# First projection, input vector and first value sums of a decode attention block on one Trainium2 core

wq is loaded in five transfers of 12-KB rows instead of two, x as one row that the TensorE turns, and the first head's value sums are issued one chunk earlier.

## Chip, cores, metric

The kernel runs on 1 core of one Trainium2 chip. The metric is the time of one execution in microseconds of device time (us), given as the median of several executions. Profiles are of one execution each.

## The reference, cut

```python
# x [1,1,640]; k_cache, v_cache [1,32,32768,192]; wq [640,6144]; wo [6144,640]; w1 [640,1536]; w2 [1536,640]; all bf16
q = (layernorm(x) @ wq).reshape(1, 1, 32, 192).transpose(0, 2, 1, 3)
p = softmax(einsum("bhqd,bhkd->bhqk", q, k_cache) * 192 ** -0.5)
h = x + einsum("bhqk,bhkd->bhqd", p, v_cache).transpose(0, 2, 1, 3).reshape(1, 1, 6144) @ wo
out = h + relu(layernorm(h) @ w1) @ w2
```

One token attends to 32,768 cached keys in each of 32 heads. Keys and values are 805 MB of the 825 MB that are read, and each of these bytes is used once.

## The kernel before

All large loads are issued by one queue (SP). A head's keys come in two loads of 6 MB (`kt[0]`, `kt[1]`), its values in four loads of 3 MB that share two buffers (`vt[0]`, `vt[1]`). A head is worked off in eight chunks: some of the keys of a chunk are turned and scored on TensorE (PE), the others are scored on VectorE (DVE); ScalarE (ACT) takes the exponentials, and PE adds up the values. `PV h, c` is the event "value sum of head h, chunk c is done" and frees a value buffer.

wq is first put into buffers that the head loop uses later: four fifths in `kt[1]`, the last fifth in `vt[1]`. So head 0's second key load waits until the query matmuls have read wq (event `att0`).

```python
wq_c = [kt[1][:, c * H * Dh:(c + 1) * H * Dh] for c in range(DT - 1)] + [vt[1][:, 0:H * Dh]]   # DT = 5

def dma_program(g):
    ...
    def keys(h, ld):
        if h > 0:
            g.wait("PV", h - 1, 4 * ld + 1)
            g.wait("scs", h - 1, 4 * ld + 3)        # VectorE's scores of these keys
        elif ld == 1:
            g.wait("att0")
        load(kt[ld][:], rows(k_hd, h, P * JK * ld, JK), f"dk{ld}", "k", h, ld)

    def vals(h, ld):
        ...
        elif ld > 1:
            g.wait("PV", h, 2 * ld - 3)             # value load 2 waits for sum 1
    ...
    n = (DT - 1) * H * Dh
    load(kt[1][:], wq_view[:, 0:n], "dwq0", "wq", 0)                       # 48-KB rows
    load(vt[1][:, 0:H * Dh], wq_view[:, n:n + H * Dh], "dwq1", "wq", 1)    # 12-KB rows
    for h in range(LAST):
        keys(h, 0); ...; vals(h, 0); keys(h, 1); vals(h, 1); vals(h, 2)    # cut to the order of head 0
        ...

def act_start(g):
    g.do(lambda: act.dma_start(out=x_row[:], in_=A_x.rearrange("b s (c p) -> (b s c) p", p=P)), "dx", ("x",), by=16)
    g.do(lambda: act.dma_start(out=x_pc[:], in_=A_x.rearrange("b s (p c) -> (b s p) c", p=P)), "dx2", ("x_pc",), by=16)
    ...

def queries(g):
    for c in range(DT):
        if c == 0 or c == DT - 1:
            g.wait("wq", min(c, 1))
        calls = [mmul(o_ps[0:HE, 2 * h + e:2 * h + e + 1], wq_c[c][:, h * Dh + e:(h + 1) * Dh:2],
                      ln_t["ln1"]["xn"][:, c:c + 1], ...) for h in range(H) for e in range(2)]   # 64 of 96 columns
        ...

SUMS = ((), (-2,), (-1,), (0, 1), (), (2,), (3,), (4, 5))   # which value sums follow the transposes of chunk c
def pe_head(g, h, turn=None):
    for c in range(NC):
        transposes(g, h, c)
        ...
        for d in SUMS[c]:
            if d >= 0:
                values(g, h, d)
            elif h > 0:
                values(g, h - 1, NC + d)
        scores_pe(g, h, c)
        ...
```

The softmax here doesn't subtract the row's maximum and nothing guards it: scores larger than these inputs give would overflow.

## Time and profile before

| | before |
|---|---|
| median of the first three runs | 1930.16 us (1930.06 to 1931.16) |
| span of the profiled run | 1927.6 us |
| PE, VectorE, ACT busy | 81%, 81%, 50% |
| share of the main DMA queue | 99.4% |
| rate from 100 to 1880 us | 433 GB/s |
| rate from 40 to 52 and from 68 to 80 us | 228 and 280 GB/s |

The prediction shows the lines behind this table. The table of stretches for each window gives every engine's busy time, the granted clock of TensorE (the part of full speed that it was allowed), the DMA share and the rate.

### The profile page before, as it was taken

How to read it: one execution, taken by the hardware profiler on the slowest of the kernel's cores; microseconds unless marked ns; L12 is line 12 of the kernel's file. 1: busy time of each engine (PE TensorE's matmuls, PEld its weight loads, DVE VectorE, ACT ScalarE, POOL GpSimd, SP SyncE). 2: the span in 40 equal slices, each digit the busy share in tenths (PEclk: the TensorE clock that was granted, in tenths of full speed). 3: DMA queues.
4: the chain of work that ended last, by engine and by line, in shares of the span. 5: the costliest groups of instructions: out<-in, count | busy, mean ns of one | idle time of the engine just before them, and what ended most of it. 6: DMA issues, size and time to landing. Idle time of an engine off the chain costs nothing.

```text
span 1927.6 us, 36148 instructions
## 1 busy us (share of the span) xinstructions
PE 1562.3 (81%) x15900; PEld 1102.7 (57%) x15900; DVE 1560.0 (81%) x732; ACT 956.8 (50%) x2000; POOL 1.0 (0%) x6
## 2 busy tenths in 40 slices
PE   5887887888878878779788778788798797787887
PEld 5655555655655555556556556555565565555565
DVE  0988887987878878789788879888788787897895
ACT  0654544544554545545455445545455454554463
POOL 0000000000000000000000000000000000000000
PEclk9888888778788788888788888888887887987898
DMA  8999999999999999999999999999999999999998
GB/s 360 392 433 428 438 432 427 440 429 431 439 428 434 438 428 438 433 428 437 433 429 437 430 432 437 430 435 435 429 438 432 429 438 429 432 438 428 433 433 356
DMA packets 33818, 825.29 MB, mean 428 GB/s; under 512 B 3716, under 2 KB 5252, under 8 KB 8708
## 3 DMA queue, kind: packets, MB, share of 16 engines
q1 hardware_dynamic: 33642, 824.98, 99.4%
q8 instruction: 15, 0.25, 0.0%
q14 instruction: 7, 0.06, 0.0%
q10 hardware_dynamic: 154, 0.00, 0.0%
HBM read 824.97 MB, written 0.00 MB: 428 GB/s over the span
## 4 chain that ended last, share of the span: by engine, by line
DMA 55%; PE 32%; DVE 7%; ACT 5%; SPq 1%; issue 1%; POOLq 0%; DVEq 0%; ACTq 0%
DMA kt<-in_A_k_cache_dram 53%; PE o_ps L369 18%; PE tp L388 9%; ACT kT L610 5%; PE sp L369 3%; DVE pr L691 3%; DVE sc L694 3%; SPq L230 1%; DMA x_pc<-in_A_x_dram 1%; DMA w_s<-in_B_w_dram 1%; PE attT L369 1%; PE mm L369 0%; POOLq L351 0%; DVEq L65 0%; ACTq L642 0%
## 5 line engine op out<-in xcount | busy, mean ns | idle before, releaser
L691 DVE TENSOR_TENSOR pr<-kt,qb 128x2304 f32<-128x2304 bf16 (+2 forms) x257 | 755.9, 2941 | 292.8 <-POOLq L326 243.5
L610 ACT COPY kT<-tp 128x1024 bf16<-128x1024 bf16 (+1 forms) x899 | 817.6, 989 | 299.0 <-PE tp L388 297.2
L388 PE MATMUL tp<-ident_f,kt 128*128 128x128 f32 x3459 | 584.2, 337 | 234.2 <-POOLq L351 232.7
L694 DVE TENSOR_REDUCE sc<-pr 128x12 f32<-128x2304 f32 (+2 forms) x257 | 755.3, 2939 | 8.9
L388 PEld LDWEIGHTS tp<-ident_f,kt 128*128 128x128 f32 x3459 | 508.4, 175 | 241.1 <-POOLq L351 238.0
L369 PE MATMUL o_ps<-vt,pB 128*2 128x384 bf16 x2286 | 460.7, 352 | 5.2 <-POOLq L351 4.4
L369 PE MATMUL o_ps<-vt,pA 128*2 128x384 bf16 x1778 | 330.6, 326 | 0.0
L616 ACT ACTIVATE pB<-sp 128x20 bf16<-128x20 f32 (+2 forms) x258 | 47.8, 185 | 568.0 <-PE sp L369 568.0
L369 PEld LDWEIGHTS o_ps<-vt,pB 128*2 128x2 bf16 x2286 | 187.6, 88 | 230.2 <-issue 92.0
L369 PEld LDWEIGHTS sp<-qm,kT 128*128 128x128 bf16 x6918 | 192.4, 98 | 178.2 <-ACT kT L610 134.7
L369 PE MATMUL sp<-qm,kT 128*128 128x2 bf16 x6918 | 214.3, 164 | 98.2 <-ACT kT L610 96.9
L369 PEld LDWEIGHTS o_ps<-vt,pA 128*2 128x2 bf16 x1778 | 150.1, 84 | 142.8 <-issue 5.1
L625 ACT ACTIVATE pA<-sc 128x12 bf16<-128x12 f32 (+2 forms) x257 | 53.4, 208 | 39.1 <-DVEq L65 38.3
L616 ACT ACTIVATION_READ_ACCUMULATOR pB<-sp 128x1 f32 x258 | 50.2, 195 | 0.0
L625 ACT ACTIVATION_READ_ACCUMULATOR pA<-sc 128x1 f32 x257 | 48.9, 190 | 0.0
L705 DVE TENSOR_SCALAR o_pair<-o_ps,rec 2x384 bf16<-2x384 f32 x32 | 19.4, 605 | 6.3 <-PE o_ps L369 1.7
L369 PE MATMUL o_ps<-xn_ln,kt 128*96 128x1 bf16 (+1 forms) x316 | 22.4, 208 | 0.0
L369 PEld LDWEIGHTS o_ps<-xn_ln,kt 128*96 128x96 bf16 (+1 forms) x316 | 22.2, 176 | 0.1
L369 PE MATMUL mm<-st_ln,mean_mat 128*128 128x2 f32 (+1 forms) x4 | 0.9, 304 | 19.7 <-DVE sq_ln L722 19.4
L369 PE MATMUL attT<-oT,wo_s 128*128 128x1 bf16 x465 | 16.3, 164 | 0.3 <-DVE oT L715 0.3
L369 PEld LDWEIGHTS mm<-dsums,ones_mat 128*128 128x128 f32 x64 | 15.9, 305 | 0.3 <-issue 0.3
L715 DVE TENSOR_SCALAR oT<-mm,odd 128x3 bf16<-128x3 f32 x32 | 7.1, 223 | 10.5 <-PE mm L369 8.1
(69 smaller groups left out, 156.0 us busy)
## 6 DMA issues: line engine op xcount, KB each, us to landing
vt<-in_A_v_cache_dram SPq DMA_DIRECT2D x126, 3072.0 KB, 19.0
kt<-in_A_k_cache_dram SPq DMA_DIRECT2D x62, 6144.0 KB, 32.6
kt<-in_A_k_cache_dram SPq DMA_DIRECT2D x3, 3072.0 KB, 20.3
wo_s<-in_A_wo_dram SPq DMA_DIRECT2D x16, 480.0 KB, 9.5
kt<-in_A_wq_dram SPq DMA_DIRECT2D x1, 6144.0 KB, 17.5
vt<-in_A_v_cache_dram SPq DMA_DIRECT2D x2, 1536.0 KB, 13.5
kt<-in_A_k_cache_dram SPq DMA_DIRECT2D x1, 1920.0 KB, 27.9
kt<-in_A_v_cache_dram SPq DMA_DIRECT2D x2, 960.0 KB, 18.3
```

Of the source, the lines that this page charges most:

```text
L230: g.do(lambda: nc.sync.dma_start(out=dst, in_=src), sem, label, by=16)
L369: return lambda: pe.matmul(o, lhsT=w, rhs=r, **kw)
L388: calls.append(lambda b=b, o=o: pe.transpose(out=dst[:, b, :], in_=src[:, o:o + 2 * P].bitcast(f32), identity=ident_f[:]))
L610: g.do(lambda: act.copy(out=kT[c % 2][:, b0:b0 + nb, :], in_=src[:, 0:nb, :].bitcast(bf16)), "act_pe", ("cp", h, c, k))
L616: g.do(lambda: act.activation(out=pB[c % NB][:, 0:jp], in_=sp[:, 0:jp], func=F.Exp, scale=SCALE, accum_out=dsums[:, 2 * c + 1:2 * c + 2]), ...
L625: g.do(lambda: act.activation(out=pA[c % NB][:, 0:jd], in_=sc[c % NC][:, 0:jd], func=F.Exp, scale=SCALE, accum_out=dsums[:, 2 * c:2 * c + ...
L691: g.chain(lambda: dve.tensor_tensor(out=pr[:, 0:j1 - j0, :], in0=src[:, (off + j0) * Dh:(off + j1) * Dh].rearrange("p (j d) -> p j d", d=D ...
L694: g.chain(lambda: dve.reduce_sum(out=sc[c % NC][:, j0:j1], in_=pr[:, 0:j1 - j0, :], axis=X), "dve")
L705: g.do(lambda: dve.tensor_scalar_mul(out=o_pair[:, :, 1, :], in0=o_ps[0:2, 0:2 * Dh].rearrange("q (i d) -> q i d", i=2), scalar1=rec[0:2, ...
L715: g.do(lambda: dve.tensor_scalar_mul(out=oT[:], in0=mm[:, 0:3], scalar1=odd[:]), "dve_pe", ("oTc", h))
```

## The change

The intent is to start the queries sooner. x then no longer has to arrive in 128 pieces of 10 bytes, the query matmuls begin on the first fifth of wq, and head 0 frees its value buffer one chunk sooner.

```diff
-    x_row = sbuf("x_row", [DT, P], bf16)
-    x_pc = sbuf("x_pc", [P, DT], bf16)
+    x_row = sbuf("x_row", [1, D], bf16)
+    xx = sbuf("xx", [P, 2 * DT], f32)
+    x_pc, x_col = xx[:, 0:DT], xx[:, DT:2 * DT]
 ...
-                g.wait("PV", h - 1, 4 * ld + 1)
+                g.wait("PV", h - 1, 2 if h == 1 and ld == 0 else 4 * ld + 1)
 ...
-        n = (DT - 1) * H * Dh
-        load(kt[1][:], wq_view[:, 0:n], "dwq0", "wq", 0)
-        load(vt[1][:, 0:H * Dh], wq_view[:, n:n + H * Dh], "dwq1", "wq", 1)
+        for c in range(DT):
+            load(wq_c[c], wq_view[:, c * H * Dh:(c + 1) * H * Dh], f"dwq{c}", "wq", c)
 ...
-            if c == 0 or c == DT - 1:
-                g.wait("wq", min(c, 1))
+            g.wait("wq", c)
 ...
-            for d in SUMS[c]:
+            for d in (SUMS[c] if h > 0 or c > 5 else ((), (0,), (1,), (), (2,), ())[c]):
 ...
     def pe_start(g):
         g.wait("identf")
+        g.wait("x")
+        cols = [x_row[0:1, c:D:DT] for c in range(DT)] + [x_row[0:1, c * P:(c + 1) * P] for c in range(DT)]
+        pe_group(g, [mmul(mm[:, i:i + 1], col, ident_b[0:1, 0:1], start=True, stop=True) for i, col in enumerate(cols)],
+                 ("xT",), "pe_dve")
         pe_norm(g)
         g.wait("xn", "ln1")
-        g.wait("x")
-        pe_group(g, [lambda: pe.transpose(out=mm[:, 0:4].bitcast(bf16)[:, 0:DT], in_=x_row[:], ...)], ("xT",), "pe_dve")
 ...
-        g.do(lambda: act.dma_start(out=x_row[:], in_=A_x.rearrange("b s (c p) -> (b s c) p", p=P)), "dx", ("x",), by=16)
-        g.do(lambda: act.dma_start(out=x_pc[:], in_=A_x.rearrange("b s (p c) -> (b s p) c", p=P)), "dx2", ("x_pc",), by=16)
+        g.do(lambda: act.dma_start(out=x_row[:], in_=A_x.rearrange("b s d -> (b s) d")), "dx", ("x",), by=16)
 ... (VectorE: one copy of the ten columns to xx; the norm reads its first five)
```

The longer wait of head 1's first key load is a consequence of the third part. With the old order, sum 1 followed the transposes of chunks 0 to 3, which read `kt[0]`. Now only sum 2 does.

More of the change, by code (lines that the diff above doesn't have):

```diff
@@ L182 @@
     odd = sbuf("odd", [P, 1], f32)
-    x_col = sbuf("x_col", [P, DT], f32)
     h_col = sbuf("h_col", [P, DT], f32)
@@ L219 @@
     names = ["pool_pe", "act_pe", "dve_pe", "act_dve", "dve_act", "dve", "dve_row", "pe_dve", "pool_row", "pool_dve", "pool_act", "pe_act", "pe", "dve_sp"]
-    names += [f"dk{i}" for i in range(NK)] + [f"dv{i}" for i in range(NV)] + ["dwq0", "dwq1", "dwo", "dx", "dx2", "dout"]
+    names += [f"dk{i}" for i in range(NK)] + [f"dv{i}" for i in range(NV)] + ["dwo", "dx", "dout"] + [f"dwq{i}" for i in range(5)]
     names += [f"dke{i}" for i in range(4)] + ["dvh"] + [f"dve{i}" for i in range(4)] + ["dw1"] + [f"dw2_{i}" for i in range(3)]
@@ L530, in pe_start @@
         g.wait("identf")
+        g.wait("x")
+        cols = [x_row[0:1, c:D:DT] for c in range(DT)] + [x_row[0:1, c * P:(c + 1) * P] for c in range(DT)]
+        pe_group(g, [mmul(mm[:, i:i + 1], col, ident_b[0:1, 0:1], start=True, stop=True) for i, col in enumerate(cols)],
+                 ("xT",), "pe_dve")
         pe_norm(g)
         g.wait("xn", "ln1")
-        g.wait("x")
-        pe_group(g, [lambda: pe.transpose(out=mm[:, 0:4].bitcast(bf16)[:, 0:DT], in_=x_row[:],
-                                          identity=ident_b[0:DT, 0:DT])], ("xT",), "pe_dve")
         queries(g)
@@ L539, in pe_start @@
         g.wait("qe")
-        g.wait("x_col")
         q_spread(g, 0)
@@ L720, in dve_norm @@
         t = ln_t[tag]
-        g.chain(lambda: dve.reduce_sum(out=t["st"][:, 0:1], in_=col[:], axis=X), "dve_row")
-        g.chain(lambda: dve.scalar_tensor_tensor(out=t["sq"][:], in0=col[:], scalar=1.0, in1=col[:], op0=A.mult,
+        g.chain(lambda: dve.reduce_sum(out=t["st"][:, 0:1], in_=col, axis=X), "dve_row")
+        g.chain(lambda: dve.scalar_tensor_tensor(out=t["sq"][:], in0=col, scalar=1.0, in1=col, op0=A.mult,
                                               op1=A.mult, accum_out=t["st"][:, 1:2]), "dve_row", ("st", tag))
@@ L731, in dve_norm @@
         g.wait("rs", tag)
-        g.do(lambda: dve.tensor_scalar(out=t["xn"][:], in0=col[:], scalar1=t["mv"][:, 0:1], scalar2=t["rs"][:],
+        g.do(lambda: dve.tensor_scalar(out=t["xn"][:], in0=col, scalar1=t["mv"][:, 0:1], scalar2=t["rs"][:],
                                        op0=A.subtract, op1=A.mult), "dve_pe", ("xn", tag))
@@ L740, in dve_start @@
         g.do(lambda: dve.tensor_copy(out=ident_f[:], in_=ident_b), "dve_pe", ("identf",))
-        g.wait("x_pc")
+        g.wait("xT")
+        g.chain(lambda: dve.tensor_copy(out=xx[:], in_=mm[:, 0:2 * DT]), "dve_row")
         dve_norm(g, "ln1", x_pc)
-        g.wait("xT")
-        g.chain(lambda: dve.tensor_copy(out=x_col[:], in_=mm[:, 0:4].bitcast(bf16)[:, 0:DT]), "dve_row", ("x_col",))
     def dve_head(g, h):
@@ L765, in dve_end @@
         t = ln_t["ln2"]
-        g.chain(lambda: dve.scalar_tensor_tensor(out=h_col[:], in0=attT[:, 0:DT], scalar=1.0, in1=x_col[:], op0=A.mult,
+        g.chain(lambda: dve.scalar_tensor_tensor(out=h_col[:], in0=attT[:, 0:DT], scalar=1.0, in1=x_col, op0=A.mult,
                                                  op1=A.add, accum_out=t["st"][:, 0:1]), "dve_row", ("h_col",))
```

## The prediction

> **What bounds the kernel now.** I read the page first, then the table of stretches (busy time by engine, granted clock, DMA share and rate in windows that I chose), then the timeline of the queue that issues transfers, and last the chain of waits and the landing times for the start.
>
> ```profile
> PE 1562.3 (81%) x15900; PEld 1102.7 (57%) x15900; DVE 1560.0 (81%) x732; ACT 956.8 (50%) x2000; POOL 1.0 (0%) x6
> ...
> q1 hardware_dynamic: 33642, 824.98, 99.4%
> ```
>
> No compute engine is over 81% busy, while one DMA queue, which carries all the keys and values, fills 99.4% of the sixteen DMA engines' span. The time is set by how long 825 MB take, plus the stretches in which nothing is moved. The table of stretches finds those:
>
> ```profile
> 2.00:40.00 38.00, 19.16 (x234) 19.09 (x235) 1.93 (x13) 1.51 (x2) 0.00 (x0) 1.00 1.01 425
> 40.00:52.00 12.00, 11.04 (x115) 10.71 (x114) 3.30 (x2) 3.40 (x7) 0.00 (x0) 1.00 0.60 228
> 52.00:68.00 16.00, 10.29 (x123) 9.34 (x123) 15.49 (x6) 11.28 (x24) 0.00 (x0) 0.68 0.98 421
> 68.00:80.00 12.00, 9.56 (x106) 6.53 (x106) 11.54 (x5) 5.87 (x14) 0.00 (x0) 0.93 0.72 280
> 80.00:100.00 20.00, 19.77 (x187) 12.31 (x185) 16.96 (x6) 10.37 (x21) 0.00 (x0) 0.87 1.01 431
> 100.00:1880.00 1780.00, 1455.48 (x14709) 1019.98 (x14709) 1482.97 (x671) 906.21 (x1893) 0.00 (x0) 0.84 1.00 433
> ```
>
> The last column is GB/s, the one before it the DMA share. From 100 to 1880 us the rate is flat at 433 with a share of 1.00. Only two stretches fall short: 40 to 52 us (228 GB/s) and 68 to 80 us (280 GB/s). Against 433 they lose 12 x 205/433 = 5.68 us and 12 x 153/433 = 4.24 us; the recovery after the first (52 to 68, 421 GB/s) loses 16 x 12/433 = 0.44 us more. That is **10.4 us of holes in all**, and the most that a change at the start can win. The ramp of the first 38 us (38 x 8/433 = 0.7 us) is there either way.
>
> The issue timeline says what each hole waits for:
>
> ```profile
> 1.90 0.42 SPq L230 DMA_DIRECT2D kt<-in_A_k_cache_dram  x1
> 2.37 0.77 SPq L230 DMA_DIRECT2D vt<-in_A_v_cache_dram  x1
> 47.34 0.33 SPq L230 DMA_DIRECT2D kt<-in_A_k_cache_dram  x1
> 47.71 26.13 SPq L230 DMA_DIRECT2D vt<-in_A_v_cache_dram  x2
> 73.88 0.43 SPq L230 DMA_DIRECT2D wo_s<-in_A_wo_dram  x1
> 74.36 0.43 SPq L230 DMA_DIRECT2D kt<-in_A_k_cache_dram  x1
> ```
>
> The second key load of head 0 is issued only at 47.34, because its buffer holds wq until the query matmuls have read it; everything issued earlier has landed by 2.37 + 42.7 = 45.1 us (issue plus the landing time that the list of issues gives). The next wait lasts to 73.9 us: the third value load needs the buffer that value sum 1 of head 0 releases, and the stream issued at 47 us ran out at 47.71 + 25.7 = 73.4 us. The chain of waits shows why the queries are late:
>
> ```profile
> 1.54 17.35 DMA x_pc<-in_A_x_dram
> ...
> 21.40 0.18 PE mm L534
> 21.58 25.70 PE o_ps L369 x320
> ```
>
> 1.2 KB of x take 17.35 us to land; the normalisation takes the 2.5 us to 21.4, and 320 query matmuls take 25.70 us. The wq load, landing beside x, would not let them start earlier either:
>
> ```profile
> kt<-in_A_wq_dram SPq DMA_DIRECT2D x1, 6144.0 KB, 17.5
> vt<-in_A_wq_dram SPq DMA_DIRECT2D x1, 1536.0 KB, 20.6
> ```
>
> Issued at 0.96, its 6 MB are there at 18.5 us, as one semaphore.
>
> **What the Trainium skill says.** "DMA: Bandwidth & Descriptors", section "Queues, rings and completion order": each engine goes round-robin between the queues that have work, switching only at packet boundaries. This fits the 17.35 us for 1.2 KB: 128 elements of 10 bytes over 16 engines are 8 turns, and if each waits for one 48-KB row of wq (49,152 B at 433/16 = 27 GB/s: 1.82 us) that is 14.5 us plus start and landing. The same page, "Where 436 GB/s comes from", puts the ceiling of the fabric at 435 GB/s; the trace's 433 is at it, so nothing but the holes can be won. Its section "Why small descriptors are slow (HBM only)" names a fixed cost per packet; no trace of before shows 12-KB rows at length except the fifth of wq, so I estimate them as 1 to 2% slower than 48-KB rows. "TensorE: Matmul & The Clock Gate", section "LDWEIGHTS (loading the stationary operand)": the load goes by columns, not rows. The trace has a weight load of 5 x 128 at 0.10 us and its matmul at 0.18 us, so a one-row load should cost the same 0.10 us.
>
> **The change part by part.**
>
> *x.* One row, one issue, taken in few packets rather than 128. The ACT queue issues it at 0.91, ahead of wq by a hair; I expect it to land by 2 to 3.5 us (estimate: at most one or two 12-KB rows of 0.46 us ahead of it). Ten pairs of 0.10 us load and a matmul are 1.0 to 1.3 us after the identity at 2.78; one copy is 0.2 us; then the same chain from the first sum to xn, 21.35 - 18.91 = 2.44 us. xn is ready near 6.5 to 7 us instead of 21.35.
>
> *wq.* Each fifth is 1.57 MB or 3.63 us at 433 GB/s. Since four fifths landed at 18.5, the first lands near 18.5 - 3 x 3.63 = 7.6 us, the others at 11.2, 14.9, 18.5, 22.2. Each fifth's 64 matmuls take 25.70/5 = 5.14 us, slower than the loads, so after the first no wait remains: the queries run from 7.6 to 33.3 us (before: 47.28), at the granted clock of 1.00 that the table shows for the whole of 2 to 52 us. The buffer is released at 33.5 and the second key load is issued there, 11.6 us before the stream of 45.1 us runs dry. **Hole 1 (5.68 + 0.44 us) closes.** The 12-KB rows cost 1 to 2% of 14.5 us: +0.2 us.
>
> *Stream of head 0 after this.* Key load 0 lands as before, 1.90 + 35.7 = 37.6, with the 0.2 of wq 37.8; values 0 at 45.3, keys 1 (6.29 MB, 14.5 us) at 59.8, values 1 (7.3 us) at 67.1. Compute of head 0, which began at 48.67, begins at 38.0 on the landing of the keys.
>
> *Value sums one chunk earlier.* In before, sum 1 ended at 73.47, which is 24.8 us after VectorE's first product at 48.67. With the old order it would now end at 38.0 + 24.8 = 62.8, already 4 us ahead of 67.1. With the new order it follows VectorE's second chunk (done 60.7 - 48.67 = 12.0 us after the start, so at 50) and one group of transposes (3.4 us) and 16 matmuls (2.6 us): about 56 us, a reserve of 11 us. **Hole 2 (4.24 us) closes**, and I hold that the early start of head 0 suffices for it; this part is insurance. It also makes the next head's first key load wait for sum 2, which waits for values 1 at 67.1: with 2.9 us of matmuls it is issued near 70.3, while the stream then has values 2 to 74.4 and wo (0.49 MB, 1.1 us) to 75.5. A reserve of 5 us, the smallest.
>
> *Later loads of head 0.* In before, value load 3 was issued at 91.3 and the next two near 99.2, that is 13 and 21 us after the scores of chunk 4 (78.30). From 70.3 this gives 83 and 91; the stream, with keys to 90.0 and values to 97.3, has not run dry. From head 1 on the order is unchanged, and the transfers were 1.00 busy.
>
> *Sum.* -5.68 - 0.44 - 4.24 + 0.2 = -10.2 us. PE, VectorE and ACT do practically the same work and lie off the path. 1930.16 - 10.2 = **1920.0 us**.
>
> **The rivals.** (1) *A hole takes the place of one removed*: key load of head 1 is now tied to sum 2 and so to the landing of values 1. For it: all margins are estimates, engines finish a load up to 2 us apart, and the clock drops to 0.5 in places. Against it: 5 us of reserve. If hole 2 survives in part: 1921 to 1924.5. (2) *PE becomes the bound at the start*: if the queries ran at half clock they would take 51 us, end at 59, and hole 1 would grow to some 14 us: 1934. Against it: the granted clock is 1.00 throughout the queries of before. (3) *The transfers' gain is given back later*, the compute being unable to follow: PE waits for key landings (230 us of idle over the heads in the groups of lines), about 7 us a head; so it can follow, and I give this little. (4) *12-KB rows are slow*: at 400 GB/s wq would cost 1.4 us more: 1921.5. Upward, the landing-based view of the holes (a landing interval of 21.0 us for keys 1 after values 0 where 14.5 are needed) would make them 6.5 + 4.2 us, so 1919.5.
>
> **Range and chances.** The three runs of before span 1.1 us, so the range is one of mechanism: full success 1918.5 to 1921, a partial new hole to 1923. 8 in 10: 1918.0 to 1923.0. Two per cent is 38.6 us, and only 11 can be won: faster 0.01, same 0.98, slower 0.01.
>
> **What would show it.** In the table of stretches, 40 to 52 and 68 to 80 us both near 430 GB/s; xn before 7.5 us; the query matmuls starting near 7.6 and ending near 33; the second key load issued near 33.5, value load 2 near 56, head 1's keys near 70; steady rate 433 unchanged. I am wrong if a window under 420 GB/s remains between 30 and 110 us, if the queries start over 3 us late yet the time stands (they have 11 us to spare), or if the stretch after 110 us loses its 433.

## More of the kernel before

A share of busy time over the whole span cannot show a hole of a few microseconds; windows of 10 to 20 us can. A packet's bytes are booked where it starts, so a single window can read a little high and its neighbour low.

## The result

The changed kernel takes 1919.72 us (median of four runs, 1919.31 to 1920.48), against 1930.11 us for the kernel before in the same rounds (1929.6 to 1931.16). The ratio is 0.9946, with a 95% interval of 0.9929 to 0.9963. Ratios here are the mean time of one kernel's fast runs over that of the other's of the same rounds, so not quite the ratio of the medians quoted. The gain of 10.4 us lies within two per cent.

The table of stretches of the changed kernel, in the windows that the prediction uses (the first line names the columns):

```profile
core 0: us, PE busy (x) PEld busy (x) DVE busy (x) ACT busy (x) POOL busy (x), PEclk, DMA share, GB/s
2.00:40.00 38.00, 29.91 (x353) 29.61 (x354) 4.30 (x14) 2.94 (x7) 0.00 (x0) 1.00 1.01 426
40.00:52.00 12.00, 10.71 (x108) 7.83 (x107) 11.64 (x5) 9.38 (x18) 0.00 (x0) 1.00 1.08 466
52.00:68.00 16.00, 9.42 (x98) 6.93 (x96) 15.36 (x7) 8.83 (x17) 0.00 (x0) 0.85 0.94 405
68.00:80.00 12.00, 9.94 (x99) 6.60 (x98) 11.64 (x5) 7.15 (x15) 0.00 (x0) 0.78 1.03 430
80.00:100.00 20.00, 17.62 (x198) 11.82 (x197) 14.59 (x7) 11.06 (x25) 0.00 (x0) 0.99 0.99 426
100.00:1880.00 1780.00, 1453.84 (x14706) 1018.60 (x14705) 1482.98 (x673) 904.68 (x1888) 0.00 (x0) 0.84 1.00 433
```

Both holes are gone. The 466 and 405 of neighbouring windows are the booking of packets at their start: over both together the rate is (12 x 466 + 16 x 405)/28 = 431. The steady part is at 433 as before. Over the window from 40 to 100 us the profile gives 357 GB/s before and 429 after. That is 60 x (433 - 357)/433 = 10.5 us lost before and 0.6 us after: the difference of 9.9 us is nearly the whole gain.

The queue that issues the transfers, changed kernel (start, time including the wait in front of a group's later members, what was issued):

```profile
3.91 0.45 SPq L230 DMA_DIRECT2D vt<-in_A_v_cache_dram  x1
32.92 0.33 SPq L230 DMA_DIRECT2D kt<-in_A_k_cache_dram  x1
33.30 20.88 SPq L230 DMA_DIRECT2D vt<-in_A_v_cache_dram  x2
54.22 0.43 SPq L230 DMA_DIRECT2D wo_s<-in_A_wo_dram  x1
71.10 0.33 SPq L230 DMA_DIRECT2D kt<-in_A_k_cache_dram  x1
82.14 8.14 SPq L230 DMA_DIRECT2D vt<-in_A_v_cache_dram  x2
```

The second key load of head 0 leaves at 32.92 instead of 47.34 us, and value load 2 (the second of the pair, just before wo) near 53.8 instead of 73.5. Head 1's keys leave at 71.10.

The chain of waits at the start, changed kernel:

```profile
0.97 6.03 DMA kt<-in_A_wq_dram
...
7.13 25.73 PE o_ps L368 x320
```

The landing of the first fifth of wq releases the queries, where before the landing of x did. Then 320 matmuls run without a wait. The timeline shows x off that chain:

```profile
2.83 0.49 PE L368 MATMUL mm<-wide,x_row 1*128 1x1 bf16 x10 [2.83 <-DVE ident_f L737]
...
5.64 0.29 DVE L729 TENSOR_SCALAR xn_ln<-xx,mv_ln,rs_ln 128x5 bf16<-128x5 f32 x1
```

The ten one-row matmuls wait for the identity and not for x. The normalised vector is ready at 5.93 us, 1.2 us ahead of wq.

### The profile page after: what moved, and what is told of

It is laid out like the page before. It is cut to its first block, busy times and chain, and to the rows that moved or that the text cites. A ratio compares the mean times of both kernels' runs of the same rounds, so it can differ in the third digit from the quotient of the medians.

```text
span 1918.7 us, 36168 instructions
## 1 busy us (share of the span) xinstructions
PE 1560.2 (81%) x15909; PEld 1099.7 (57%) x15909; DVE 1560.0 (81%) x732; ACT 957.9 (50%) x2000; POOL 1.0 (0%) x6
## 4 chain that ended last, share of the span: by engine, by line
DMA 55%; PE 30%; DVE 8%; ACT 5%; SPq 1%; issue 1%; POOLq 0%; DVEq 0%; ACTq 0%
DMA kt<-in_A_k_cache_dram 52%; PE o_ps L368 17%; PE tp L387 9%; ACT kT L608 5%; DVE pr L688 4%; DVE sc L691 4%; PE sp L368 3%; DMA vt<-in_A_v_cache_dram 2%; SPq L230 1%; DMA w_s<-in_B_w_dram 1%; PE attT L368 1%; PE mm L368 0%; DMA kt<-in_A_wq_dram 0%; DVEq L65 0%; POOLq L350 0%
## 5 line engine op out<-in xcount | busy, mean ns | idle before, releaser
L368 PEld LDWEIGHTS mm<-dsums,ones_mat 128*128 128x128 f32 x64 | 15.4, 295 | 0.3 <-issue 0.3
L696 DVE TENSOR_REDUCE rec<-mm 128x1 f32<-128x20 f32 x32 | 5.7, 179 | 12.0 <-PE mm L368 7.5
## 6 DMA issues: line engine op xcount, KB each, us to landing
kt<-in_A_k_cache_dram SPq DMA_DIRECT2D x1, 1920.0 KB, 28.3
```

The costliest lines, as they stand in the source:

```text
L368: return lambda: pe.matmul(o, lhsT=w, rhs=r, **kw)
L696: g.chain(lambda: dve.reduce_sum(out=rec[:, 0:1], in_=mm[:, 0:2 * NCM], axis=X), "dve")
```

## The experiments

The theory: the time is the transfers' time plus the holes in their stream, and the change closes two holes. Hole 1 is the wait of head 0's second key load for the queries; hole 2 is the wait of value load 2 for sum 1. The rivals: one part does all the work; the start of the compute itself is on the path; the holes only move. The parts were tried singly and in pairs, the queries were delayed by three doses, and two kernels tried to mend the end of the stream. All twelve runs were correct, each with five timed runs.

| kernel | median us | kernel before, same rounds | gained us | GB/s 40 to 100 us | lost there: 60 x (433 - rate)/433 |
|---|---|---|---|---|---|
| sums only | 1926.21 | 1930.16 | 4.0 | 385 | 6.7 |
| x only | 1927.15 | 1930.16 | 3.0 | 378 | 7.6 |
| wq only | 1921.42 | 1930.16 | 8.7 | 420 | 1.8 |
| x and wq (old sums) | 1919.68 | 1930.16 | 10.5 | 427 | 0.8 |
| the change, again | 1920.34 | 1930.68 | 10.3 | 427 | 0.8 |
| the change, 64 matmuls more | 1919.77 | 1930.68 | 10.9 | 425 | 1.1 |
| the change, 192 matmuls more | 1926.99 | 1930.68 | 3.7 | 378 | 7.6 |
| w2 in long rows | 1920.92 | 1930.68 | 9.8 | - | - |
| x and sums | 1922.80 | 1930.97 | 8.2 | 405 | 3.9 |
| wq and sums | 1919.23 | 1930.97 | 11.7 | 429 | 0.6 |
| the change, 128 matmuls more | 1921.52 | 1930.97 | 9.5 | 415 | 2.5 |
| w2 in pairs of rows | 1919.54 | 1930.97 | 11.4 | - | - |

Before loses 10.5 us in that window by the same reckoning. In each row gained plus lost comes to between 10.5 and 12.3 us, so nearly all of each kernel's gain is found in the DMA stream between 40 and 100 us. Runs of one kernel differ by some 1 to 2 us, and gains by under 1 us are not told apart here. The three groups of runs (their medians of the kernel before differ) were taken on three different chips, so across groups it is the gain that is compared.

### The earlier sums alone

```diff
 kernel before, with
-                g.wait("PV", h - 1, 4 * ld + 1)
+                g.wait("PV", h - 1, 2 if h == 1 and ld == 0 else 4 * ld + 1)
-            for d in SUMS[c]:
+            for d in (SUMS[c] if h > 0 or c > 5 else ((), (0,), (1,), (), (2,), ())[c]):
```

> Only the earlier value sums; wq in two loads and x as before. Theory (each hole has its own cause): the queries still end near 47.3 us, so hole 1 stays (second key load issued near 47.3), but sum 1 of head 0 is done near 66 us, ahead of the 73.4 us at which the stream runs dry, so hole 2 closes: 1930.1 - 4.2 = 1925.9 us (1925 to 1927). Rival (the moved sums only shift the wait to head 1's keys, which now wait for sum 2): 1929 to 1931 us.

Measured: 1926.21 us, ratio 0.9978 (0.9965 to 0.9992). The stretches of this kernel:

```profile
40.00:52.00 12.00, 11.40 (x117) 10.91 (x116) 3.14 (x2) 3.24 (x6) 0.00 (x0) 1.00 0.59 223
...
68.00:80.00 12.00, 7.42 (x97) 5.51 (x97) 11.54 (x5) 7.76 (x17) 0.00 (x0) 1.00 1.08 461
```

Hole 1 is as before (223 against 228 GB/s), and hole 2 is gone (461 against 280). The holes have separate causes. Each can be closed without the other, and the longer wait of head 1's keys (issued at 77.11) does not replace hole 2.

### The change without the earlier sums

```diff
 changed kernel, with
-            for d in (SUMS[c] if h > 0 or c > 5 else ((), (0,), (1,), (), (2,), ())[c]):
+            for d in SUMS[c]:
 and the wait of head 1's keys as before
```

> The whole change but the earlier value sums. Theory (the sums are insurance, head 0 starting 10.6 us earlier closes hole 2 by itself): value load 2 issued near 62.8 us, ahead of the 67.1 us at which the stream runs dry; 1920 us (1919 to 1921), the same as the change. Rival (the earlier sums are needed for hole 2): 4.2 us more, 1924 us.

Measured: 1919.68 us, ratio 0.9950 (0.9936 to 0.9963). Its issue timeline:

```profile
33.37 29.81 SPq L230 DMA_DIRECT2D vt<-in_A_v_cache_dram  x2
63.22 0.43 SPq L230 DMA_DIRECT2D wo_s<-in_A_wo_dram  x1
```

Value load 2 leaves just before wo, at 62.8 us, and the stream lasts to 66.6 (33.30 + 33.3 in the changed kernel). Where head 0 starts early, the earlier sums gain nothing that these runs can tell.

### x alone

```diff
 changed kernel, with wq in two loads and the old sums:
-        for c in range(DT):
-            load(wq_c[c], wq_view[:, c * H * Dh:(c + 1) * H * Dh], f"dwq{c}", "wq", c)
+        load(kt[1][:], wq_view[:, 0:n], "dwq0", "wq", 0)
+        load(vt[1][:, 0:H * Dh], wq_view[:, n:n + H * Dh], "dwq1", "wq", 1)
```

> Only x as one row with ten one-row matmuls; wq in two loads, old sums. Theory (the 6-MB wq load lands at 18.5 us as one semaphore and keeps the queries from starting): xn ready near 6 us, queries from 18.6 to 44.3, so the chain that ends in value load 2 moves only 3.0 us forward, hole 1 shrinks and hole 2 grows: 1930.1 - 3.0 = 1927.1 us (1926 to 1928). Rival (the landing of x alone held the queries): 1920 to 1922 us.

Measured: 1927.15 us, ratio 0.9985 (0.9971 to 0.9998). The chain of waits at its start:

```profile
0.96 17.47 DMA kt<-in_A_wq_dram
18.57 25.75 PE o_ps L369 x320
```

With x there early, the queries wait for 6 MB of wq behind one semaphore. They start 3.0 us earlier than before, and 3.0 us are gained. Hole 1 shrinks (354 GB/s from 40 to 52 us against 228). Hole 2 stays (279 GB/s from 68 to 80 us against 280) and starts sooner (394 GB/s from 52 to 68 us against 421), as the keys and values ahead of it were issued earlier.

### wq alone

```diff
 kernel before, with
+        for c in range(DT):
+            load(wq_c[c], wq_view[:, c * H * Dh:(c + 1) * H * Dh], f"dwq{c}", "wq", c)
 and g.wait("wq", c) in the queries; x and the sums as before
```

> Only wq in five loads; x in its two loads of before (128 elements of 10 bytes), old sums. Theory (x waits one wq row per turn, so 12-KB rows make its 8 turns four times shorter): x lands near 7 us instead of 18.9, xn near 9.5, queries end near 35, both holes close: 1920 us (1919 to 1921.5), and the new x path is worth nothing beside this. Rival (the 17 us are a fixed cost of 128 small elements): x lands near 18.9 us, queries end near 47, 1930 us.

Measured: 1921.42 us, ratio 0.9955 (0.9942 to 0.9969). The rival falls: x is quicker without having been touched. But x landed at 9.95 us and not near 7, and the time is 1.4 us over the expectation. The chain of waits:

```profile
1.53 8.42 DMA x_pc<-in_A_x_dram
...
12.65 25.70 PE o_ps L368 x320
```

The queries end at 38.35 us instead of 32.86, and with the old sums value load 2 is issued only at 64.8 us. The loads before it land by 38.77 + 28.1 = 66.9. The stretches of this kernel around that moment show the price all the same:

```profile
60.00:62.00 2.00, 2.00 (x14) 1.01 (x12) 1.97 (x2) 0.45 (x1) 0.00 (x0) 1.00 1.01 426
62.00:64.00 2.00, 2.00 (x15) 1.04 (x13) 1.96 (x1) 0.00 (x0) 0.00 (x0) 1.00 1.03 442
...
64.00:68.00 4.00, 3.17 (x44) 2.45 (x42) 3.76 (x2) 2.46 (x7) 0.00 (x0) 1.00 0.80 270
```

From 64 to 68 us the rate is 270 GB/s, which loses 4 x (433 - 270)/433 = 1.5 us, the excess over the expectation. The load was issued 2.1 us before the earlier ones had all landed, and that was not early enough. From 64 to 65 us, as it is issued, the DMA share is already down to 0.58 (246 GB/s). I read this as engines that do not finish together, the first of which find nothing queued; the views quoted here show the mean over the engines only.

The queue view tells a good part of why x was slow before. In the kernel before, between 6 and 16 us (queue, packets, MB, share; q1 carries wq, q10 carries x):

```profile
q1 hardware_dynamic: 93, 4.57, 105.5%
q10 hardware_dynamic: 94, 0.00, 0.5%
```

In this stretch there is one packet of x for each row of wq, and 94 packets in 10 us over 16 engines are one per engine in 1.70 us, close to the 1.82 us that a 48-KB row takes at 27 GB/s. With 12-KB rows the same view of this kernel, from 6 to 10 us, has:

```profile
q1 hardware_dynamic: 144, 1.57, 95.0%
q10 hardware_dynamic: 129, 0.00, 1.8%
```

That is again about one for one, and 3.4 times as fast. The turns are not the whole of it: x's elements begin to move only some 4 us after their issue, in both kernels (see the part on why the prediction was right).

### wq and the sums; x and the sums

```diff
 wq and sums: the kernel of "wq alone" with the earlier sums
 x and sums: the changed kernel with wq in two loads
```

> wq in five loads and the earlier sums, x as before. Theory (wq alone took 1921.4 us because value load 2 was issued at 65.2 us while the first of the engines ran dry near 64.5; the earlier sums bring it to near 57): the 1.5 us go, 1920 us (1919.2 to 1920.8). Rival (the small x elements slow the wq stream itself by as much): 1921.4 us again.

Measured: 1919.23 us, ratio 0.9941 (0.9927 to 0.9954). Value load 2 leaves before 56 us, and the stretch from 40 to 100 us is at 429 GB/s. So x in 128 elements of 10 bytes, landing 9 us after its issue, costs nothing that these runs can tell once the sums come early. The x path is not needed for the gain.

> x as one row and the earlier sums, wq in two loads. Theory: queries end near 44.3 us as in the run of x alone, hole 1 shrinks to (issue 44.4 - landing 45.1) + 3.9 = 3.2 us from 6.1 and hole 2 closes: 1919.7 + 3.2 - 0.2 = 1922.7 us (1922 to 1923.7). Rival (the parts simply add: x alone -3.0, sums alone -4.0): 1923.2 us; the two can't be told apart by time, only by the rate in the stretches 40 to 52 and 68 to 80 us. Rival (wq in five loads is worth nothing beyond this): 1920 us.

Measured: 1922.80 us, ratio 0.9960 (0.9947 to 0.9974). From 40 to 52 us it reads 341 GB/s, from 68 to 80 us 419: hole 1 remains in part and hole 2 is closed, as the theory has it. Without wq in five loads 2.2 us of the gain of the change are missing, and 3.5 us of that of "wq and sums".

### The queries delayed

The change was run again as a base:

> The change itself again, as the base for the runs beside it: 1919.7 us (1919 to 1920.8).

Measured: 1920.34 us, ratio 0.9946 (0.9933 to 0.9960). Then extra matmuls of the queries' kind, whose result is not used, were put ahead of the queries:

```diff
 changed kernel, in queries():
+        g.wait("wq", 0)
+        for i in range(N):      # N = 64, 128, 192
+            g.do(mmul(sp[0:HE, 0:1], wq_c[0][:, (i % H) * Dh:(i % H + 1) * Dh:2], ln_t["ln1"]["xn"][:, 0:1], start=True, stop=True))
```

> The change with 64 extra matmuls of the queries' kind (right result) ahead of the queries, 64 x 80 ns = 5.1 us on PE. Theory (only the holes of the DMA stream count, and the queries have some 11 us to spare): queries end near 38 us, second key load issued near 38 us while the stream lasts to 45 us; 1920 us, no change. Rival (the start of the compute is on the path): 5 us more, 1925 us.

Measured: 1919.77 us, ratio 0.9944 (0.9930 to 0.9958). The key load leaves at 38.12 instead of 32.92, and 5.2 us of delay cost nothing.

> The change with 128 extra matmuls (10.3 us) ahead of the queries. With 192 the key load was issued at 48.56 us and 7.1 us were lost, so loss = issue - 41.5 once it is positive. Theory: issue near 43.3, a little before the last landing at 45.1 but after the fastest engines have run dry: 1.8 us lost, 1921.7 us (1920.5 to 1922.5). Rival (no loss until the last landing): 1919.9 us.

Measured: 1921.52 us, ratio 0.9952 (0.9939 to 0.9966). The key load leaves at 43.25. The loss is 1.8 us against the first median of the change, 0.9 us if the gains over the kernel before are compared, and 2.3 us against "wq and sums" of the same rounds. The rival (no loss before the last landing at 44.8) does not fit the rate either: 376 GB/s from 40 to 52 us against 448 with 64 matmuls (the first line is of 64, the second of 128):

```profile
40.00:52.00 12.00, 10.71 (x106) 8.44 (x105) 11.64 (x5) 8.82 (x17) 0.00 (x0) 1.00 1.04 448
```

```profile
40.00:52.00 12.00, 10.44 (x113) 9.30 (x113) 7.24 (x3) 7.46 (x14) 0.00 (x0) 1.00 0.94 376
```

> The same with 192 extra matmuls, 15.4 us. Theory: queries end near 48.3 us, past the end of the stream at 45.1; hole 1 comes back, larger than in the kernel before by the 1.0 us that they end later: 6.1 + 1.0 = 7.1 us more; hole 2 stays closed as the earlier sums are in: 1926.8 us (1926 to 1928). Rival (all of the delay counts): 1935 us; rival (holes don't matter): 1920 us.

Measured: 1926.99 us, ratio 0.9981 (0.9967 to 0.9995), 6.7 us over the change of the same rounds. The stretches of this kernel:

```profile
40.00:52.00 12.00, 11.73 (x129) 11.64 (x129) 2.10 (x1) 2.17 (x5) 0.00 (x0) 1.00 0.48 177
52.00:68.00 16.00, 14.71 (x152) 9.94 (x151) 15.46 (x7) 10.95 (x23) 0.00 (x0) 1.00 1.00 430
```

The key load leaves at 48.56, 1.2 us later than in the kernel before, and hole 1 is back and larger (177 against 228 GB/s). PE worked all through it. Of 15.4 us more work, the first ten cost about 2 us at most (0.9 to 2.3) and the next five cost five. This is the shape of a reserve that is used up, not of work on the path.

### The end of the stream

The last loads are w1 and w2, in rows of 3,072 and 1,280 bytes, and the rate over the last 12 us of the stream is only 373 GB/s.

```diff
 changed kernel, long rows:
-            load(w2_s[:, c0:c1], B_w2.rearrange("(c p) n -> p c n", p=P)[:, c0:c1], ...)
+            load(w2_s[:, c0:c1], B_w2.rearrange("(p c) n -> p c n", p=P)[:, c0:c1], ...)
-        w1_s[:, c, f * P:(f + 1) * P]
+        w1_s[:, c, f:Dff:FT]                                # 12 apart
 pairs of rows: "(c p b) n -> p c (b n)" with b=2, and w1 read 2 apart
```

> The change with w2 laid out so that a partition reads adjoining rows of HBM (long rows instead of 1,280-byte ones), the hidden units permuted to match by a strided read of w1. Theory (the end of the stream, at 373 GB/s over its last 12 us in the changed kernel against 433 in the steady part, suffers from short rows): 0.5 to 1 us less, 1919 us. Rival (the strided weight reads cost the 60 matmuls of the end as much): 1919.7 us or more.

Measured: 1920.92 us, ratio 0.9951 (0.9937 to 0.9964): no gain. Timeline lines of TensorE show why, first the changed kernel (its second run), then this one:

```profile
1909.26 1.65 PE L368 MATMUL o_ps<-xn_ln,kt 128*128 128x1 bf16 x60
1911.28 0.93 PE L368 MATMUL attT<-h1T,w_s 128*128 128x1 bf16 x30 [0.36 <-ACT h1T L665]
1912.38 1.24 PE L368 MATMUL attT<-h1T,w_s 128*128 128x1 bf16 x30 [0.18 <-DMA w_s<-in_B_w_dram]
```

```profile
1908.81 3.77 PE L368 MATMUL o_ps<-xn_ln,kt 128*128 128x1 bf16 x60
1912.94 1.76 PE L368 MATMUL attT<-h1T,w_s 128*128 128x1 bf16 x60 [0.36 <-ACT h1T L665]
```

The 60 matmuls on w1 take 3.77 us instead of 1.65, and the matmuls on w2 then wait for them (by way of ACT) and no longer, as the second half of them did, for w2's landing. The cost of the strided read is on the path.

> The change with w2 in rows of 2,560 bytes (pairs of adjoining rows), w1 read with a stride of 2 elements. With long rows w2 had landed 1.0 us earlier, but the 60 matmuls on w1 at a stride of 12 took 3.77 us instead of 1.65 and came on the path. Theory: half of the landing gain (0.5 us) is kept and the stride of 2 costs nothing (the score matmuls read keys at that stride at 30 ns each): 1919.4 us against 1919.9, at the edge of what can be told. Rival (any stride costs): h1 takes well over 1.65 us and the time is 1920 us or more.

Measured: 1919.54 us, ratio 0.9942 (0.9928 to 0.9955). At a stride of 2 the matmuls on w1 take 1.68 us, so that stride is free. But the landing gain was overrated. From the issue of w1 to the landing of the last piece of w2, the two profiles of the change have 23.2 and 23.7 us, and this kernel 23.0; the long rows have 23.0 as well. The 1.0 us in the expectation came from landing times whose zero was not the same in the two traces. The time can't be told from that of the change, and no version here clearly beats it.

## Why the prediction was right

The prediction of 1920.0 us met 1919.72. That the two differ by only 0.3 us is in part chance, as the same kernel took 1920.34 us in later rounds. Its steps held in this way:

- **What bounds the kernel.** The holes of the DMA stream were put at 10.4 us, and the change gained 10.4. The delays show the rest of the claim: PE could be given 5 us of extra work at the start for nothing.
- **x.** The row and its ten matmuls were estimated at 1.0 to 1.3 us and took 0.49, since the pairs overlap; xn came at 5.93 us instead of 6.5 to 7. Neither matters, as wq landed later.
- **wq.** The queries ran from 7.13 to 32.86 us, predicted 7.6 to 33.3. The first fifth landed at 7.0 (0.97 + 6.03), not 7.6. The rate of 64 matmuls per 5.14 us and the absence of further waits held.
- **Stream of head 0.** Keys 1 left at 32.92 (predicted 33.5), value load 2 near 53.8 (56), head 1's keys at 71.10 (70.3, where the terms that the prediction gives, 67.1 + 2.9, make 70.0). Value load 3 left at 82.14 and head 1's second key load at 90.33 (83 and 91).
- **The earlier sums as insurance.** Confirmed by the run without them: 1919.68 us, value load 2 at 62.8 us as worked out. The reserve was overrated, though. The prediction has the stream last to 67.1 and speaks of 4 us; an issue 3.8 us ahead of the last landing (62.8 against 66.6) cost nothing that can be told, but the wq-only run loses 1.5 us with one 2.1 us ahead. So at least the last 2 of those 4 us were no reserve.
- **What each part is worth.** The prediction credited x and wq together with hole 1. The runs show that wq in five loads does most of it, because it also speeds up the small x loads. Alone it gains 8.7 us; the pair without it gains 8.2. The new x path and the earlier sums can stand in for each other: with wq, either one gives 1919.2 to 1919.7 us.
- **The 17.35 us for x.** The prediction explains them by eight turns of 1.82 us, 14.5 us, plus start and landing. The records bear out the length of a turn (1.70 us) but not the sum. After the ten packets of x's first load, the queue of x has 144 packets: nine for each engine and not eight (128 are the elements; what the other 16 are is not shown). The first of them starts at 6.2 us, 4.7 us after the issue. From 6 to 16 us 94 start, beside 48-KB rows; of the last 50, all but two start after 17 us, beside the 12-KB rows of wq's last fifth. So the turns took some 12.5 us and not 14.5, and the rest is mostly the start of 4.7 us, which the prediction named without a size. I left it out once more when I had x land near 7 us in the wq-only run: there the first element starts at 5.4 us, 3.9 us after the issue, the last by 9.6 us, and x has landed at 9.95. These 4 us are not made of turns, as each engine had moved two 48-KB rows by then in the one run and about six 12-KB rows in the other. Their cause stays open.
- **The rivals.** No hole moved to head 1's keys (430 GB/s from 68 to 80 us), the queries did not run slower, and 433 GB/s held to 1880 us. One sign of being wrong that the prediction named is there by the letter, a window under 420 GB/s (405 from 52 to 68 us). From 40 to 68 us the rate is 431, so I take it for the booking of packets; the sign was set too tight for single windows. The estimate of 0.2 us for 12-KB rows is below what can be told: the first 38 us ran at 426 GB/s, before at 425.

What stays open: how the loss begins engine by engine when a load is issued about 2 us before the end of the stream, why the 128 elements of x begin to move only some 4 us after their issue, and whether pairs of w2 rows gain the few tenths that their profile hints at.

## What to carry to other kernels

In a kernel bound by its transfers, look for the windows in which nothing moves, and ask of each hole which issue waited, and for what. Two holes in a row must be tried apart: narrowing the first can close the second (x and wq without the sums) or leave it as it was (x alone). Split a first load so that work can start on its first piece, and note that its row length also sets how long a small load on another queue waits for its turns.

## What the Trainium skill lacked or had wrong

- "DMA: Bandwidth & Descriptors", section "Queues, rings and completion order": it says that an engine drains a whole packet, typically 9 to 17 descriptors, before it turns to the next queue. Here the packet records alternate about one row for one small element (93 and 94 in 10 us with 48-KB rows, 144 and 129 in 4 us with 12-KB rows). How many descriptors such a record holds is not shown, so this does not contradict the page. What follows from its rule, that a small load's landing grows with the other queue's row length (17.35 us against 8.42 us for the same x), is not spelled out on any page that I read.
- The same page, section "Latency and other measured facts", gives about 0.6 us to the first byte of such a transfer. For x in 128 elements of 10 bytes it was 4.7 us (6.2 against 1.54, kernel before) and 3.9 us (5.4 against 1.53, wq alone). Nor does it say how early the next load must be queued to keep the stream full: an issue 2.1 us before the last landing lost 1.5 us, and one 3.4 us after it (48.56 against 3.95 + 41.2 = 45.2 in that run) lost 6.7 us.
- "TensorE: Matmul & The Clock Gate", section "Weight-path perf modes — Fast Weight Load (FWL) and DoubleRow": no gap, but a check. The page makes full 128 columns a condition of the quick load, and the trace agrees. The 96-column query matmuls run at 80 ns each (20.61 us for 256), 128-column ones at 28 ns (1.65 us for 60), and also at 28 ns at the queries' step of 2 elements between columns (1.68 us for 60). At a step of 12 they take 63 ns (3.77 us for 60); that section does not speak of this cost, but it is not lacking from the skill, as another page covers reads with a step.
